# Dealing the seven VectorE steps of a float64 conversion differently over a unit, and testing the exponent with ScalarE's Square

## The chip, the cores and the metric

One core of one Trainium2 chip runs the program. The metric is the device time of one execution in microseconds (us); lower is better.

## What is computed

The reference is pooled attention, then a mixture of eight experts, then a layer with softplus. Cut to what matters:

```python
x = attention(q, mean_pool(k), mean_pool(v))          # x: 2304 x 512
P = sinkhorn(x @ moe_w_gate)                           # shares, 8 rounds
for e in range(8):
    out += P[:, e:e+1] * (np.maximum(x @ w1[e], 0) @ w2[e])
h = out @ moe2_w_in                                    # 512 x 2048
y = (np.maximum(h, 0) + np.log1p(np.exp(-np.abs(h)))) @ moe2_w_out
```

The two weights of the last layer arrive as float64. The kernel reads them as pairs of 32-bit words and turns them into float32 on the chip; that is the conversion which is changed here.

## The kernel before

**Precision and products.** Every float32 operand is split in a high and a low part, and each product is three matmuls (hi·hi, lo·hi, hi·lo; `three`, L797). The products of a unit are formed by a scheme with seven products in place of eight: A11, A22, S2, S1, A12, S3 and S4.

**Units and phases.** The 2304 tokens are worked on in three groups of 768. A unit is 256 columns of the hidden layer; an expert has four. There are six phases: the expert layer for the three groups (32 units each) and then the softplus layer for the three groups (8 units each). In the first phase and in the softplus phases each unit goes by itself (`first`, `second`). In the second and third phases (`TWICE`) units go in pairs, an even and an odd one: `first_twice` makes the hidden values of a unit, and the second product too is formed with seven products for the pair (`form_product`, from `second_twice`). The order in which the instructions are issued is written by hand, and each engine works its own list in that order: first(2d), second(2d−1), first(2d+1), second(2d), and so on.

**first_twice (L848).** It issues products A11, A22, S2, S1, A12 and S3, and later S4. After each of the first six it calls `between(k)`, k = 0 to 5. ScalarE copies A11's result to `za` between k = 0 and 1. VectorE forms `u1` (`u` in the trace) from S2's bank after S1 has been issued. S3 is accumulated onto that same bank, so S3 can't start before `u1` has been formed. After S3, VectorE makes three sums (`za` and two `p`), then comes `between(5)`. The posts of the unit follow in `second_twice`: `shared` (L889: relu times the shares), the high parts on ScalarE (L892) and the low parts on VectorE or GpSimd (L896), and sums (L845, L846).

**The conversion.** `from_float64` is a generator. One chunk is 128 x 512 values. `f` is the raw data: `up` the high words, `dn` the low words. Seven VectorE steps with a tile `a` (`da`), a tile `r` and a tile `t` (`dt`): shift and mask (L1258), put in sign and top exponent bit (L1260), shift the low word (L1264 or L1272), compare the magnitude and multiply (L1266), mask out the exponent (L1268), scale the low part (L1273), add (L1276). ScalarE's Abs (L1261) makes the magnitude in place in `f`, for the comparison of L1266. Each call of `convert()` runs the generator to its next `yield`, so a `yield` is where the next step waits for the next call. A `yield True` ends the chunk; then `done` stores `t`, and fetches the next raw data into `f`, at the next call of `settled()`.

In the pair phases `a` and `r` are the two halves of one double bank of PSUM on the side that the second products use (`not in_c`). `convert()` is called from `between(k)` of odd units, at k = 0 to 5, and only once a chunk is open after k = 0. So a chunk begins at k = 0 of an odd unit and its data is stored and the next fetched in the even unit that follows. In the other phases (`in_c`) the tiles are single banks, and `convert()` is called from `hook()`.

Tiles named "ex" (where `t` lives) have two buffers, which some remainders (`xl`) use as well.

Of the kernel before, what the change touches and what calls it, by code (L numbers as in the profile page):

```python
# [12 lines left out]
AF = mybir.ActivationFunctionType  # L13
ALU = mybir.AluOpType
# [5 lines left out]
def attention_moe_softplus_kernel(  # L20
# [12 lines left out]
    nc = tc.nc  # L33
# [46 lines left out]
    def bank(name, kind="y", dt=F32):  # L80
        if kind not in banks:
            kind = away[0] or ""
        if kind in halves:
            return banks[kind].tile([P, 2, 512], dt, tag=f"two{kind}", name=name)[:, 0, :]
        return banks[kind].tile([P, 512], dt, tag=f"bank{kind}", name=name)
# [1126 lines left out]
    def widths():  # L1212
        for u in range(NU2):
            o = u * US
            src = w_in[:, 2 * o:2 * (o + US)].rearrange("(c p) (f w) -> p c f w", p=P, w=2)
            for s in range(2):
                yield src[:, 2 * s:2 * s + 2], v1[u][:, 2 * s:2 * s + 2, :]
            src = w_out[o:o + US, :].rearrange("(c p) (d w) -> p c d w", p=P, w=2)
            for s in range(2):
                yield src[:, s:s + 1], v2[u][:, s:s + 1, :]  # L1220
# [6 lines left out]
    def from_float64():  # L1227

        ts, stt = nc.vector.tensor_scalar, nc.vector.scalar_tensor_tensor
        every = list(widths())  # L1230
        unread = list(enumerate(every))
        loaded = []

        def fetch(at):
            if unread and at < len(f64_t):
                i, (src, _) = unread.pop(0)
                _, c, f, w = src.shape
                raw = f64_t[at].rearrange("p (c f w) -> p c f w", c=c, w=w)
                nc.sync.dma_start(raw, src)
                loaded.append((i, at, raw))  # L1240

        for at in range(len(f64_t)):
            fetch(at)
        for _ in range(4):
            yield True
        while loaded:
            i, at, raw = loaded.pop(0)
            up = raw[:, :, :, 1].rearrange("p c f -> p (c f)")
            dn = raw[:, :, :, 0].rearrange("p c f -> p (c f)")
            size = lambda x: x.bitcast(F32)  # L1250
            in_c = "c" in banks
            if in_c:
                a = bank("da", "c", U32)
            else:
                both = banks[away[0]].tile([P, 2, 512], U32, tag=f"two{away[0]}", name="da")
                a, r = both[:, 0], both[:, 1]
            t = tpool.tile([P, up.shape[1]], F32, tag="ex", name="dt")
            ts(a, up, 3, 0x3FFFFFF8, op0=ALU.logical_shift_left, op1=ALU.bitwise_and)  # L1258
            yield False
            stt(a, up, 0xC0000000, a, op0=ALU.bitwise_and, op1=ALU.bitwise_or)  # L1260
            nc.scalar.activation(size(up), size(up), AF.Abs)  # L1261
            yield False
            if not in_c:
                ts(r, dn, 1, None, op0=ALU.logical_shift_right)  # L1264
            yield False
            stt(size(a), size(up), 1.125 * 2.0 ** -15, size(a), op0=ALU.is_ge, op1=ALU.mult)  # L1266
            yield False
            ts(t.bitcast(U32), a, 0xFF800000, None, op0=ALU.bitwise_and)  # L1268
            yield False
            if in_c:  # L1270
                r = bank("dr", "y", U32)
                ts(r, dn, 1, None, op0=ALU.logical_shift_right)  # L1272
            stt(t, r, 2.0 ** -51, t, op0=ALU.mult, op1=ALU.mult)  # L1273
            if in_c:
                yield False
            nc.vector.tensor_tensor(t, size(a), t, op=ALU.add)  # L1276

            def done(i=i, at=at, t=t):
                nc.sync.dma_start(every[i][1].rearrange("p c f -> p (c f)"), t)
                fetch(at)  # L1280
                converted[0] += 1

            settle.append(done)
            yield True


    conversion = from_float64()
    between_chunks = [True]

# [446 lines left out]
```

## Time and profile before

| | |
|---|---|
| median of 3 runs | 1968.52 us (1967.92 to 1969.78) |
| profiled execution | 1970.1 us, its span 1968.3 us |
| TensorE (PE) | busy 1936.8 us |
| VectorE (DVE) | busy 1465.7 us |
| GpSimd (POOL) | busy 1475.1 us |
| ScalarE (ACT) | busy 977.0 us |
| granted TensorE clock | 0.998 of full speed |

The span runs from the first to the last instruction of the profiled execution. Busy time says how much of it an engine had an instruction in work; a matmul's end is modelled, so a start that comes late against the pace of its neighbours says more than the busy time. In the rows below, what stands in square brackets is the time that the engine sat idle ahead of the instruction and the instruction that ended it.

### The profile page before, as it was taken

To read this page: it belongs to the slowest core of one execution; us is meant where nothing else is said; L and a number is where in the kernel's file an instruction comes from. 1 tells how busy PE (TensorE), PEld (TensorE's weight loads), DVE (VectorE), ACT (ScalarE), POOL (GpSimd) and SP (SyncE) were. 2 spreads that over 40 slices of the span, in tenths; PEclk is the share of its full clock that TensorE was granted. 3 is DMA by queue.
4 is the path that set the end of the run, shared out by engine and by line. 5 is a ranking of instruction groups with operands and counts; after the bars stand their busy time and mean duration, and the time that the engine had idled before them with its cause. 6 is when DMAs were issued, how large, how long until landed. Compare 5 with 4: busy or idle time off the path is not lost.

```text
span 1968.3 us, 30479 instructions
## 1 busy us (share of the span) xinstructions
PE 1936.8 (98%) x10954; PEld 1794.6 (91%) x10954; DVE 1465.7 (74%) x2339; ACT 977.0 (50%) x1777; POOL 1475.1 (75%) x1142
## 2 busy tenths in 40 slices
PE   9899999999999999999999999999999999999999
PEld 7677888888989999999999999999999988999998
DVE  6776576787667888878888879888789766556455
ACT  6545435343334545545445554454554565565542
POOL 5776667778877789778777798887787879666563
PEclk9999999999999999999999999999999999999999
DMA  7443433555547655554555655555545523523411
GB/s 198 120 147 125 144 124 135 177 166 182 179 153 262 200 164 166 166 181 152 160 172 159 214 169 163 160 170 162 186 150 158 190 85 115 202 91 115 139 65 64
DMA packets 213347, 306.56 MB, mean 156 GB/s; under 512 B 33308, under 2 KB 147532, under 8 KB 212940
## 3 DMA queue, kind: packets, MB, share of 16 engines
q1 hardware_dynamic: 203116, 290.85, 45.7%
q10 hardware_dynamic: 10080, 13.77, 1.9%
q8 instruction: 86, 1.41, 0.3%
q14 instruction: 65, 0.53, 0.1%
HBM read 239.30 MB, written 65.27 MB: 155 GB/s over the span
## 4 chain that ended last, share of the span: by engine, by line
PE 79%; DVE 14%; POOL 3%; ACT 3%; DMA 1%; issue 1%; SPq 0%; ACTq 0%; POOLq 0%; DVEq 0%
PE py L797 39%; PE p L797 36%; DVE p L889 2%; DVE g L845 2%; DVE hlo L896 2%; DVE p L845 2%; POOL w1lo L289 1%; ACT hhi L892 1%; DVE s L846 1%; DVE dt L1276 1%; PE px L522 1%; DVE dt L1273 1%; PE s L477 1%; DVE za L845 1%; DVE u L845 1%
## 5 line engine op out<-in xcount | busy, mean ns | idle before, releaser
L797 PE MATMUL p<-xhi,w1hi 128*128 128x384 f32 x1680 | 573.2, 341 | 10.0 <-DVE u L845 5.0
L797 PE MATMUL p<-xhi,w1lo 128*128 128x384 f32 x1680 | 563.7, 336 | 0.0
L797 PE MATMUL p<-xlo,w1hi 128*128 128x384 f32 x1680 | 563.5, 335 | 0.2 <-DVE xlo L1397 0.2
L289 POOL TENSOR_TENSOR w2lo<-w2raw,w2hi 128x512 fp32r<-128x512 f32 (+1 forms) x235 | 363.8, 1565 | 118.7 <-ACT w2hi L243 103.8
L289 POOL TENSOR_TENSOR w1lo<-w1raw,w1hi 128x512 fp32r<-128x512 f32 x240 | 239.3, 1019 | 232.9 <-ACT w1hi L320 232.1
L797 PEld LDWEIGHTS p<-xhi,w1hi 128*128 128x128 f32 x1680 | 315.9, 188 | 35.3 <-DVE u L845 14.3
L797 PEld LDWEIGHTS p<-xlo,w1hi 128*128 128x128 f32 x1680 | 316.0, 188 | 4.7 <-DVE xlo L1397 0.4
L797 PEld LDWEIGHTS p<-xhi,w1lo 128*128 128x128 f32 x1680 | 315.8, 188 | 0.0
L289 POOL TENSOR_TENSOR w1lo<-sums,w1hi 128x1024 fp32r<-128x1024 f32 x120 | 288.6, 2405 | 2.1 <-ACT w1hi L320 2.1
L797 PE MATMUL py<-w2hi,hhi 128*128 128x512 f32 x672 | 266.6, 397 | 5.4 <-DVE g L1117 1.6
L797 PE MATMUL py<-w2hi,hlo 128*128 128x512 f32 x672 | 263.8, 393 | 0.0
L797 PE MATMUL py<-w2lo,hhi 128*128 128x512 f32 x672 | 263.3, 392 | 0.0
L797 PE MATMUL py<-hhi,w2hi 128*128 128x384 f32 x716 | 241.4, 337 | 1.0 <-ACT whi L243 1.0
L797 PE MATMUL py<-hhi,w2lo 128*128 128x384 f32 x716 | 239.6, 335 | 0.0
L797 PE MATMUL py<-hlo,w2hi 128*128 128x384 f32 x716 | 239.5, 335 | 0.0
L845 DVE TENSOR_TENSOR g<-py,g 128x768 f32<-128x768 f32 x210 | 199.6, 950 | 50.1 <-PE py L797 50.1
L892 ACT CAST hhi<-p 128x768 fp32r<-128x768 f32 x128 | 102.6, 802 | 209.2 <-DVE p L889 174.6
L797 PEld LDWEIGHTS py<-w2hi,hhi 128*128 128x128 f32 x672 | 126.3, 188 | 36.9 <-DVE g L1132 4.5
L797 PEld LDWEIGHTS py<-w2hi,hlo 128*128 128x128 f32 x672 | 126.1, 188 | 26.9
L797 PEld LDWEIGHTS py<-w2lo,hhi 128*128 128x128 f32 x672 | 126.2, 188 | 22.2
L797 PEld LDWEIGHTS py<-hhi,w2hi 128*128 128x128 f32 x716 | 134.4, 188 | 5.1 <-DVE dt L1276 3.8
L797 PEld LDWEIGHTS py<-hhi,w2lo 128*128 128x128 f32 x716 | 134.5, 188 | 0.0
(164 smaller groups left out, 3548.1 us busy)
## 6 DMA issues: line engine op xcount, KB each, us to landing
w1raw<-in_moe_w_dram SPq DMA_DIRECT2D x96, 512.0 KB
w2raw<-td SPq DMA_DIRECT2D x128, 256.0 KB
sums<-sd SPq DMA_DIRECT2D x62, 512.0 KB
w2raw<-in_moe_w_dram SPq DMA_DIRECT2D x96, 256.0 KB
w2raw<-in_moe_w_dram SPq DMA_DIRECT2D x32, 512.0 KB
sd<-sums SPq DMA_DIRECT2D x32, 512.0 KB
td<-w2raw SPq DMA_DIRECT2D x64, 256.0 KB
xlo<-xlod SPq DMA_DIRECT2D x35, 384.0 KB
```

The costliest lines, as they stand in the source:

```text
L289: nc.gpsimd.tensor_tensor(o, a, b, op=ALU.subtract)
L477: nc.tensor.matmul(ps[:QP, j * 2 * SP:(j + 1) * 2 * SP], qT[:, j * QP:(j + 1) * QP], kb)
L522: nc.tensor.matmul(px[h * D:(h + 1) * D, :W], vp[:, h, :], aT[:, h, :])
L797: nc.tensor.matmul(ps, lhs[a], rhs[b], start=first and i == 0, stop=last and i == 2, skip_group_check=goes_on,)
L845: vadd = lambda o, x, y: nc.vector.tensor_tensor(o, x, y, op=ALU.add)
L846: vsub = lambda o, x, y: nc.vector.tensor_tensor(o, x, y, op=ALU.subtract)
L889: nc.vector.scalar_tensor_tensor(o, src, 0.0, share, op0=ALU.max, op1=ALU.mult)
L892: nc.scalar.copy(h_slot(q)[0], src)
L896: eng.tensor_tensor(lo, src, hi.bitcast(F32), op=ALU.subtract)
L1273: stt(t, r, 2.0 ** -51, t, op0=ALU.mult, op1=ALU.mult)
L1276: nc.vector.tensor_tensor(t, size(a), t, op=ALU.add)
```

## The change

In the pair phases, where a chunk had its VectorE steps dealt over six calls as 1, 1, 1, 1, 1, 2, it now has them dealt over five, as 2, 1, 2, 1, 1. In the other phases the seven steps stay dealt as they were (1, 1, 0, 1, 1, 2, 1). ScalarE's Abs, which stood behind the second step and wrote over the raw words, is replaced by a Square that is issued ahead of the first step and writes to `t`; the comparison reads `t` and compares with a squared bound. `t` is later overwritten by the masking step, as before.

```diff
+        least = (1.125 * 2.0 ** -15) ** 2 * (1 - 2.0 ** -23)
...
             t = tpool.tile([P, up.shape[1]], F32, tag="ex", name="dt")
+            nc.scalar.activation(t, size(up), AF.Square)
             ts(a, up, 3, 0x3FFFFFF8, op0=ALU.logical_shift_left, op1=ALU.bitwise_and)
-            yield False
+            if in_c:
+                yield False
             stt(a, up, 0xC0000000, a, op0=ALU.bitwise_and, op1=ALU.bitwise_or)
-            nc.scalar.activation(size(up), size(up), AF.Abs)
             yield False
             if not in_c:
                 ts(r, dn, 1, None, op0=ALU.logical_shift_right)
             yield False
-            stt(size(a), size(up), 1.125 * 2.0 ** -15, size(a), op0=ALU.is_ge, op1=ALU.mult)
-            yield False
+            stt(size(a), t, least, size(a), op0=ALU.is_ge, op1=ALU.mult)
+            if in_c:
+                yield False
             ts(t.bitcast(U32), a, 0xFF800000, None, op0=ALU.bitwise_and)
             yield False
             if in_c:
                 r = bank("dr", "y", U32)
                 ts(r, dn, 1, None, op0=ALU.logical_shift_right)
             stt(t, r, 2.0 ** -51, t, op0=ALU.mult, op1=ALU.mult)
-            if in_c:
-                yield False
+            yield False
             nc.vector.tensor_tensor(t, size(a), t, op=ALU.add)
```

## Rows read from the trace of the kernel before

**Rows 1.** The page's first part: busy time, share, instructions.

```profile
PE 1936.8 (98%) x10954; PEld 1794.6 (91%) x10954; DVE 1465.7 (74%) x2339; ACT 977.0 (50%) x1777; POOL 1475.1 (75%) x1142
```

**Rows 2.** Stretches: length, busy PE, PEld, DVE, ACT, POOL (instructions), clock, DMA share, GB/s.

```profile
1039.60:1069.60 30.00, 29.75 (x168) 29.01 (x169) 26.37 (x37) 14.40 (x24) 23.01 (x17) 1.00 0.55 171
...
1399.78:1429.19 29.41, 29.40 (x169) 29.08 (x169) 24.16 (x34) 15.73 (x27) 23.05 (x17) 1.00 0.53 174
```

**Rows 3.** Waits, whole span: us in total, times, longest us.

```profile
PEld p L797 <- DVE u L845: 14.3, 29, 0.6
...
PEld py L797 <- DVE dt L1276: 5.1, 23, 0.2
...
PE p L797 <- DVE u L845: 5.0, 21, 0.2
```

**Rows 4.** Timeline, VectorE, an odd unit with a chunk: start, us, instruction.

```profile
1052.39 0.96 DVE L845 TENSOR_TENSOR g<-py,g 128x768 f32<-128x768 f32 x1 [1.15 <-PE py L797]
1053.26 0.68 DVE L1258 TENSOR_SCALAR da<-f 128x512 uint32<-128x512 uint32 x1
1053.98 0.70 DVE L1260 SCALAR_TENSOR_TENSOR da<-f,da 128x512 uint32<-128x512 uint32 x1
1054.71 0.70 DVE L1264 TENSOR_SCALAR da<-f 128x512 uint32<-128x512 uint32 x1
1056.62 0.56 DVE L845 TENSOR_TENSOR u<-p,za 128x384 f32<-128x384 f32 x1 [1.21 <-PE p L797]
...
1059.22 1.03 DVE L845 TENSOR_TENSOR p<-p,za 128x384 f32<-128x384 f32 x2
1060.16 0.68 DVE L1273 SCALAR_TENSOR_TENSOR dt<-da,dt 128x512 f32<-128x512 uint32 x1
...
1061.49 0.96 DVE L889 SCALAR_TENSOR_TENSOR p<-p,pb 128x768 f32<-128x768 f32 x1
...
1069.00 0.55 DVE L845 TENSOR_TENSOR u<-p,za 128x384 f32<-128x384 f32 x1
```

**Rows 5.** Timeline, TensorE: start of S3, odd unit; around S3, next even unit.

```profile
1057.39 0.34 PE L797 MATMUL p<-xhi,w1hi 128*128 128x384 f32 x1
...
1069.02 0.34 PE L797 MATMUL p<-xhi,w1lo 128*128 128x384 f32 x1
1069.60 0.44 PE L797 MATMUL p<-xhi,w1hi 128*128 128x384 f32 x1 [0.25 <-DVE u L845]
1069.88 0.34 PE L797 MATMUL p<-xlo,w1hi 128*128 128x384 f32 x1
```

**Rows 6.** Timeline, VectorE, a stretch without a chunk: first post, next `u`.

```profile
1391.06 0.97 DVE L889 SCALAR_TENSOR_TENSOR p<-p,pb 128x768 f32<-128x768 f32 x1
...
1399.17 0.55 DVE L845 TENSOR_TENSOR u<-p,za 128x384 f32<-128x384 f32 x1
```

**Rows 7.** Timeline, ScalarE and VectorE: start of two odd units with a chunk.

```profile
1052.02 0.62 ACT L243 CAST whi<-w2raw 128x512 fp32r<-128x512 f32 x1 [1.45 <-DMA w2raw<-td]
1054.47 0.48 ACT L858 COPY za<-p 128x384 f32<-128x384 f32 x1 [1.83 <-PE p L797]
...
1204.43 0.68 DVE L1258 TENSOR_SCALAR da<-f 128x512 uint32<-128x512 uint32 x1
...
1205.88 0.62 ACT L243 CAST whi<-w2raw 128x512 fp32r<-128x512 f32 x1 [4.13 <-DMA w2raw<-td]
```

**Rows 8.** Groups of L1261, whole span: busy us, mean ns, idle before.

```profile
L1261 ACT ACTIVATE f<-f 128x512 f32<-128x512 f32 x32 | 21.8, 682 | 36.0 <-DVE da L1260 36.0
...
L1261 ACT ACT_TABLE_LOAD x2 | 2.6, 1283 | 0.0
```

**Rows 9.** Timeline, start of the softplus phases: VectorE, ScalarE, TensorE.

```profile
1612.39 0.70 DVE L1266 SCALAR_TENSOR_TENSOR da<-f,da 128x512 f32<-128x512 f32 x1 [0.75 <-ACT f L1261]
...
1618.81 1.28 ACT L817 ACT_TABLE_LOAD   x1 [0.98 <-DVE xl L741]
...
1624.99 0.50 PE L797 MATMUL py<-w2hi,hhi 128*128 128x512 f32 x1 [1.01 <-DVE g L1117]
```

## The prediction

> **What bounds the kernel now.** I read the engine totals first: TensorE is busy for 1936.8 us of a span of 1968.3 us [rows 1]. So only two things can change the time: the 31.5 us in which TensorE does nothing, and the places where its matmuls start later than their steady pace. Next I asked where conversion stands. The table of waits shows that in the two phases of pairs (units two by two) TensorE's weight loads wait 23 times for `dt`, the last result of a conversion chunk, 5.1 us in all, and 29 times for `u` (`u1` of `first_twice`), 14.3 us in all; its matmuls wait 21 times for `u`, 5.0 us [rows 3]. The reader is to see the counts: 23 is the number of chunks done in odd units.
>
> Then I compared stretches. A stretch from one S3 product of an even unit to the next holds 168 or 169 matmul records. With a chunk in it, it lasts 30.00 us; without, 29.41 us [rows 2]. TensorE has the same work in both, so a chunk costs TensorE 0.59 us. VectorE is busy for 26.37 us of the one and 24.16 us of the other, so it is not full in either: the chunk costs time because of where its steps stand in VectorE's queue.
>
> The timeline says where [rows 4]. Before `u` of the odd unit VectorE runs three steps (1053.26, 1053.98, 1054.71) and then idles 1.21 us until TensorE has the product. Two steps follow `u`, and two (1060.16 and the one behind it) stand after the odd unit's last sums `p`, ahead of `shared` (the first post, 1061.49), exactly where VectorE has no slack: from there to `u` of the next even unit (1069.00) it runs almost without a pause. TensorE's S3 product waits for that `u`: it starts 0.58 us after the matmul before it (1069.02, 1069.60) where 29.41 us over 169 matmuls [rows 2] make 0.17 the pace; 0.25 of it is idle, and the next start takes 0.28 [rows 5]. That is about 0.5 us lost at one place. The rest is the bank that the chunk holds until `dt` is added, and a first post 1.33 us late.
>
> **The change part by part.**
>
> *Steps dealt 2, 1, 2, 1, 1.* All seven VectorE steps remain, with their tiles. In an odd unit five stand ahead of `u` instead of three, two behind it, none after the last sums.
>
> Behind the sums [rows 4]: `shared` starts at 1060.16 instead of 1061.49, 1.33 us earlier. What that is worth at the next `u` I read from a stretch without a chunk, which has the same chain: `shared` at 1391.06, `u` at 1399.17, so 8.11 us [rows 6]. 1060.16 + 8.11 = 1068.27 against 1069.00: 0.73 us earlier. S3 started 0.60 us after `u` (1069.60 against 1069.00), so it could start at 1068.87. TensorE can't use more than it lost; the bound from both sides is nothing (another engine then holds S3) and 0.73. I take 0.59, the measured difference of the stretches, as TensorE then meets the same order as in a stretch without a chunk. The wait for `dt` (5.1 us over 23) is part of that difference and isn't added again.
>
> Ahead of `u`: two more steps must fit. A step that reads the result before it starts 0.04 us after that one ends (1053.26 + 0.68, then 1053.98); an independent one starts 0.09 before the end of its predecessor (1052.39 + 0.96, then 1053.26) [rows 4]. The comparison doesn't read the step ahead of it: 1054.71 + 0.70 − 0.09 = 1055.32. The mask does read it: 1055.32 + 0.69 + 0.04 = 1056.05. `u` is independent: 1056.05 + 0.69 − 0.09 = 1056.65 against 1056.62 now. So the idle 1.21 us is filled and `u` is 0.03 late. S3 of the odd unit starts at 1057.39 [rows 5]; with the 0.60 from above it needs `u` by 1056.79, so 0.14 us are left. I take no loss. If every added step took a dependent step's time, `u` would be another 0.26 late and S3 0.15.
>
> The two steps between `u` and the last sums replace two of the same length, so the last sums stay where they are.
>
> *Square for Abs.* One ScalarE instruction replaces another on 128x512 elements; the trace shows no Square, so its cost lies between the 0.48 us of the copy with 384 columns [rows 7] and the Abs's 0.68 with a table load of 1.28 on top [rows 8]; I take the Abs's own 0.68, the row with its shape. It no longer waits for VectorE: it reads the raw words, which were fetched in the even unit before, and writes a buffer of `t` whose last store belongs to an earlier stretch. But it now stands ahead of ScalarE's copy `za`, which would wait with it, and the comparison that reads it stands ahead of `u`. It must be ready by 1055.32, that is 2.06 us after the chunk's first step. In the stretch shown ScalarE is free after the `whi` cast at 1052.02 + 0.62 and idle until 1054.47, so Square ends near 1053.3: nothing lost. In one stretch of 21 the `whi` cast waited 4.13 us for its DMA and ended at 1206.50 [rows 7]; there Square would end near 1207.2, 2.8 after the first step (1204.43), and `u` would be 0.7 late. I charge 0.7 once.
>
> *The phases that step one by one* (bank "c") keep their dealing; only Square changes. Seven early chunks: ScalarE waited for VectorE there, but TensorE lost little. I take 0.3 us in all, with nothing and 1 us as ends. Two chunks fall at the start of the softplus phase. There Abs twice needs a table load [rows 8] and Softplus loads its table back (1618.81), 1.28 us each. TensorE then stands still for 1.01 us at 1624.99, waiting for `g` behind the late softplus [rows 9]. Without the loads: the first comparison no longer waits for Abs, which brings 0.4, an estimate from the second's 0.75; the second waited 0.75 us for it (1612.39 [rows 9]), so the chunk ends about 0.5 earlier, and with the 1.28 of the reload Softplus is 1.8 earlier. Sum 2.2 us; the ends are 0.9 (loads stay, only the wait goes) and 3.
>
> Does Square need those loads? No row shows it. The Trainium skill ("ScalarE: Activation LUTs", section "Table sets: the hidden batching unit") says that cheap functions, abs among them, are in every set. The trace disagrees: Abs behind Softplus loaded a table, 1283 ns, twice. By the page there would be nothing to save; by the row there is, if Square is served by Softplus's table.
>
> **The sum.** 21 stretches have the full pattern. 20 × 0.59 = 11.8; the one with the late cast 0.59 − 0.7 = −0.1. The two chunks at the phases' edges (23 − 21) have smaller waits: 0.7 together, an estimate from the `dt` wait (0.22) and the bank behind it. Softplus phase 2.2, early chunks 0.3. 11.8 − 0.1 + 0.7 + 2.2 + 0.3 = 14.9 us. The profiled execution took 1970.1 us with a span of 1968.3; its span would become 1953.4. The runs' median of 1968.52 lies 0.2 above that span, so 1968.5 − 15 = 1953.5 us.
>
> **The rivals.**
>
> *A. The odd unit's S3 becomes the stall.* The fit ahead of `u` has 0.14 us to spare. If steps run 0.1 slower, or Square is late in more stretches as TensorE gets faster and the w2 loads don't, S3 is 0.2 to 0.5 late in each of 21: 4 to 10 us go back, 1957.5 to 1963.5. For it: the slack is a computed one, and one cast is that late already [rows 7]. Against: the steps' rows differ by 0.02 [rows 4], and the stretches without a chunk get their `w2` loads in time at 29.41.
>
> *B. S3 of the even unit stays late.* If the posts on ScalarE or GpSimd hold it, only the `dt` waits (5.1) and the softplus phase (2.2) come off: 1961. Against: the stretches without a chunk run at 29.41 with the same posts.
>
> *C. Square loads tables as Abs did.* The 2.2 falls to 0.9: about 1955, inside the forecast's own range.
>
> *D. Slower: ScalarE holds up the comparison.* Place: the comparison, which now stands ahead of `u` and waits for Square, which waits behind ScalarE's `w2` casts and their DMAs. It decides from the point where Square ends 2.06 us after the chunk's first step; from there, less 0.14, each us late costs TensorE a us per stretch. To end slower by 4 us the 14.9 must be lost and 4 more, 0.9 us in each of 21 stretches, so Square ending 3.1 and the cast 2.4 us after the first step in all of them. The late one of the 21 ends 2.07 after it (1206.50, 1204.43) [rows 7].
>
> **Chances.** Forecast, with C in it: 0.72; A 0.12; B 0.09; D 0.03; something within 0.2% of no change beyond these, 0.04. Measurement can tell about 0.2%, 3.9 us, from no change. A and B are faster by more than that in nearly all of their span. Faster 0.90, same 0.06, slower 0.04. The likeliest case's own range is 1950.5 to 1957; for 8 in 10 I go up through A to B's 1961: 1950 to 1961. Below: the stretches can't become shorter than those without a chunk by what is shown, 21 × 0.14 more by the 0.73 bound is 3 us.
>
> **What would show it.** In the profile after: stretches between even S3 products of 29.4 to 29.5 us; five VectorE steps ahead of the odd `u` with almost no idle; `shared` straight behind the last sums; no wait of weight loads for `dt`; waits of matmuls for `u` nearly gone; one Softplus table load and none at Square. Wrong it is if the odd S3 shows a wait for `u`, or if the comparison waits for ScalarE in more than a few stretches.

## The result, and the profile after

The changed kernel takes 1954.07 us (median of 4 runs, 1953.51 to 1955.01); the kernel before, with them, 1968.36 (1967.92 to 1969.78). The ratio is 0.9919, with a 95% interval of 0.9906 to 0.9932: faster by 14.3 us, against a forecast of 15. The profiled execution took 1954.04 us with a span of 1952.3, at a granted clock of 0.999.

The first part of the page after, as [rows 1]:

```profile
PE 1928.6 (99%) x10954; PEld 1794.4 (92%) x10954; DVE 1471.4 (75%) x2339; ACT 973.6 (50%) x1773; POOL 1475.1 (76%) x1142
```

TensorE has the same 10954 matmuls; its idle time fell from 31.5 to 1952.3 − 1928.6 = 23.7 us, and the other 8 us are starts that come closer together. ScalarE has four instructions fewer, which are table loads.

Two stretches between even units' S3 products in the profile after, one with a chunk and one without, columns as in [rows 2]:

```profile
942.25:971.85 29.60, 29.59 (x168) 29.06 (x168) 26.70 (x37) 14.54 (x24) 22.98 (x17) 1.00 0.50 161
...
1387.30:1416.73 29.43, 29.42 (x168) 29.10 (x169) 24.16 (x34) 15.73 (x27) 23.05 (x17) 1.00 0.54 173
```

The stretch without a chunk is as it was; the one with a chunk fell from 30.03, which most of them last before (the 30.00 of [rows 2] is at the low end), to 29.60 and didn't reach it.

The waits after, as [rows 3]:

```profile
PEld p L797 <- DVE u L845: 14.0, 48, 0.6
...
DVE da L1268 <- ACT dt L1259: 3.2, 4, 1.0
...
PE p L797 <- DVE u L845: 0.2, 1, 0.2
```

TensorE's waits for `dt` are gone, and the matmuls' waits for `u` fell from 21 to 1. The weight loads wait for `u` 48 times instead of 29: the odd unit's `u` is now waited for too. New in the pair phases is the second row, the comparison waiting for ScalarE's Square, 4 times.

VectorE in an odd unit with a chunk and up to the next even unit's `u`, as [rows 4]:

```profile
1015.13 0.68 DVE L1260 TENSOR_SCALAR da<-f 128x512 uint32<-128x512 uint32 x1
1015.85 0.69 DVE L1263 SCALAR_TENSOR_TENSOR da<-f,da 128x512 uint32<-128x512 uint32 x1
1016.58 0.69 DVE L1266 TENSOR_SCALAR da<-f 128x512 uint32<-128x512 uint32 x1
1017.37 0.70 DVE L1268 SCALAR_TENSOR_TENSOR da<-dt,da 128x512 f32<-128x512 f32 x1
1018.10 0.69 DVE L1271 TENSOR_SCALAR dt<-da 128x512 uint32<-128x512 uint32 x1
1018.71 0.55 DVE L845 TENSOR_TENSOR u<-p,za 128x384 f32<-128x384 f32 x1
...
1021.27 1.03 DVE L845 TENSOR_TENSOR p<-p,za 128x384 f32<-128x384 f32 x2
1022.33 0.97 DVE L889 SCALAR_TENSOR_TENSOR p<-p,pb 128x768 f32<-128x768 f32 x1
1023.81 0.57 DVE L845 TENSOR_TENSOR p<-p,u 128x384 f32<-128x384 f32 x1 [0.51 <-PE p L797]
...
1030.46 0.55 DVE L845 TENSOR_TENSOR u<-p,za 128x384 f32<-128x384 f32 x1
```

Five steps stand ahead of the odd `u`, as forecast, and the first post (1022.33) stands straight behind the last sums. But `u` starts 1018.71 − 1015.13 = 3.58 us after the first step, where 3.36 was measured before and 3.39 forecast; and the step to look at is the fourth: the comparison starts 0.79 behind the shift step (1016.58, 1017.37) where 0.61 was forecast.

TensorE around the odd unit's S3 in the same stretch, as the first of [rows 5]:

```profile
1019.08 0.34 PE L797 MATMUL p<-xhi,w1lo 128*128 128x384 f32 x1
1019.31 0.44 PE L797 MATMUL p<-xhi,w1hi 128*128 128x384 f32 x1
1019.59 0.34 PE L797 MATMUL p<-xlo,w1hi 128*128 128x384 f32 x1
```

S3 starts 0.23 after its predecessor and the next matmul 0.28 after S3, where the pace is 0.17: 0.06 + 0.11 = 0.17 us lost, at a place where nothing was lost before.

### The profile page after: what moved, and what is told of

The parts are those of the page before. It is cut to its first block, busy times and chain, and to the rows that moved or that the text cites. A ratio compares the mean times of both kernels' runs of the same rounds, so it can differ in the third digit from the quotient of the medians.

```text
span 1952.3 us, 30469 instructions
## 1 busy us (share of the span) xinstructions
PE 1928.6 (99%) x10954; PEld 1794.4 (92%) x10954; DVE 1471.4 (75%) x2339; ACT 973.6 (50%) x1773; POOL 1475.1 (76%) x1142
## 4 chain that ended last, share of the span: by engine, by line
PE 90%; DVE 3%; POOL 2%; ACT 2%; DMA 1%; issue 1%; SPq 0%; ACTq 0%; DVEq 0%; POOLq 0%
PE py L797 45%; PE p L797 42%; POOL w1lo L289 1%; PE px L522 1%; PE s L477 1%; DMA vt<-in_v_dram 1%; PE pa L512 1%; DMA pb<-pd 0%; DVE p L1045 0%; POOL w2lo L289 0%; ACT w1hi L320 0%; DMA w2raw<-td 0%; PE pq L464 0%; ACT xhi L693 0%; DVE za L1045 0%
```

## The experiments

All are compared with the kernel before, timed beside them on the same chip (medians 1968.75 to 1970.1 us there). The changed kernel, run again so:

> The changed kernel once more, beside the next three on one chip: 14 to 16 us under the kernel before.

Measured 1955.46 us, 0.9926 [0.9909, 0.9943].

**Each half alone.** The dealing of before with the Square:

```diff
+            nc.scalar.activation(t, size(up), AF.Square)
             ts(a, up, 3, 0x3FFFFFF8, ...)
...
-            nc.scalar.activation(size(up), size(up), AF.Abs)
...
-            stt(size(a), size(up), 1.125 * 2.0 ** -15, ...)
+            stt(size(a), t, least, ...)
```

> The Square alone, with the steps dealt as before. If the two edits work apart, as I now read the two traces: the early chunks (about 2 us) and the softplus phase (2.3 us) come off, the stretches with a chunk stay at 30.0 us: about 1964. If freeing ScalarE from its wait for VectorE is the whole cause, 1954. If the dealing is the whole cause, 1968.

Measured 1964.74 us, 0.9969 [0.9956, 0.9981]. A stretch of it with a chunk:

```profile
1009.84:1039.88 30.04, 29.79 (x168) 29.05 (x168) 26.49 (x37) 14.44 (x24) 22.98 (x17) 1.00 0.53 160
```

The Square does nothing for the pair phases; its gain lies elsewhere. The new dealing with the Abs (after, with this edit):

```diff
-            nc.scalar.activation(t, size(up), AF.Square)
...
             stt(a, up, 0xC0000000, a, ...)
+            nc.scalar.activation(size(up), size(up), AF.Abs)
...
-            stt(size(a), t, least, ...)
+            stt(size(a), size(up), 1.125 * 2.0 ** -15, ...)
```

> The dealing alone; Abs stays, behind the second step. If the two edits work apart: stretches with a chunk of 29.6 us in place of 30.0, 21 x 0.43 = 9 us off and a little at the edges, two table loads at Abs stay: 1958 to 1960. If the Square is the whole cause, 1968; if the dealing is, 1954. Abs ends some 2.1 us after the chunk's first step and stands ahead of the copy za, so a wait of the comparison for it would show here too: then above 1960.

Measured 1961.22 us, 0.9952 [0.9939, 0.9965]. A stretch of it, and one of its waits:

```profile
1004.87:1034.47 29.60, 29.59 (x169) 29.06 (x169) 26.70 (x37) 14.54 (x24) 23.04 (x17) 1.00 0.53 161
```

```profile
ACT f L1263 <- DVE da L1262: 68.6, 26, 6.7
```

The stretch is that of the full change, though ScalarE waits longer for VectorE than before (68.6 us in 26 waits against 36.0, [rows 8]); those waits hurt mostly outside the pairs. In four of the 21 stretches in the pairs the comparison does wait for the Abs, 0.5 to 2.5 us, and they last 29.76 to 30.27. The product of the ratios is 0.9969 × 0.9952 = 0.9921, the ratio of both together 0.9919: within the intervals, the halves add.

**Abs back in the unit-by-unit phases alone.**

```diff
-            nc.scalar.activation(t, size(up), AF.Square)
+            if not in_c:
+                nc.scalar.activation(t, size(up), AF.Square)
...
+            if in_c:
+                nc.scalar.activation(size(up), size(up), AF.Abs)
```

The comparison reads `size(up)` against the old bound in these phases again.

> As after, but Abs comes back in the phases that step unit by unit (7 early chunks, 2 in the softplus phase). If Abs cost 1.8 us in the early chunks and 2.3 us at the softplus phase: 4 us more, 1958; two table loads at Abs come back. If the early difference of the two traces is scatter of the first 100 us: 2.3 us more, 1956.4. If it is hidden everywhere: 1954.

Measured 1960.71 us, 0.9948 [0.9934, 0.9961]; its span is 1958.0, 5.7 more than that of after. By the starts of the same matmuls 2.3 of it come between 331 and 500 us, in the early chunks, and 2.3 in the softplus phase; 1.0 lies at the start, ahead of any chunk. What the early chunks lose stands in the trace of before, ScalarE and TensorE:

```profile
390.49 0.66 ACT L1261 ACTIVATE f<-f 128x512 f32<-128x512 f32 x1 [6.71 <-DVE da L1260]
...
392.83 0.50 PE L797 MATMUL py<-w2hi,hhi 128*128 128x512 f32 x1 [0.54 <-DVE g L1132]
...
394.98 0.50 PE L797 MATMUL py<-w2hi,hhi 128*128 128x512 f32 x1 [0.49 <-DVE g L1132]
```

The Abs sat 6.71 us in ScalarE's queue waiting for VectorE's second step; the relu casts `hhi` stood behind it, and TensorE waited twice, about half a us each, for the `g` that follows them. In after the Square waits for no VectorE step and these two waits are gone.

**Why the odd `u` is late.** Theory: `a` and `r` are halves of one tile, so the comparison, which reads and writes `a`, waits until the shift step has written `r`. Rival: the five steps are slow for another reason. A tile of its own for `r`:

```diff
-                a, r = both[:, 0], both[:, 1]
+                a = both[:, 0]
+                r = tpool.tile([P, up.shape[1]], U32, tag="ex", name="dr")
```

> As after, but the shifted low word r goes to an SBUF tile of its own, not to the other half of the double bank that holds a. If the comparison starts 0.79 us after the r step because both are halves of one tile: it starts 0.1 to 0.18 earlier, u at 3.41 to 3.5 us after the first step in place of 3.59, the odd unit's S3 loses some 0.05 us in place of 0.19: 21 x 0.13 = 2.7 us less, about 1951.5. If the gap only comes from the comparison's second wait (for ScalarE), nothing changes: 1954.

Measured 1999.5 us, 1.0151 [1.0133, 1.0169]. This was a miss on both sides: 45 us slower than after. The shift step now reads and writes SBUF alone. Its group, then VectorE, GpSimd and TensorE around the first long one:

```profile
L1267 DVE TENSOR_SCALAR dr<-f x23: 418/421/9780, 633.3 to 1563.6; 128x512 uint32<-128x512 uint32 x23
```

```profile
721.41 8.09 DVE L1267 TENSOR_SCALAR dr<-f 128x512 uint32<-128x512 uint32 x1
...
729.42 0.68 DVE L1269 SCALAR_TENSOR_TENSOR da<-dt,da 128x512 f32<-128x512 f32 x1
```

```profile
719.44 3.80 POOL L289 TENSOR_TENSOR w2lo<-w2raw,w2hi 128x512 fp32r<-128x512 f32 x3
...
726.88 2.34 POOL L289 TENSOR_TENSOR w1lo<-sums,w1hi 128x1024 fp32r<-128x1024 f32 x1
```

```profile
731.35 0.69 PE L797 MATMUL p<-xhi,w1hi 128*128 128x384 f32 x1 [6.96 <-DVE u L845]
```

The median shift takes 0.42 us, less than in PSUM (0.69), but five of the 23 take 8.1 to 9.8. The first long one starts while GpSimd works through seven instructions back to back (719.44 to 729.22) and ends at 729.50, 0.28 after the last of them. TensorE stands still for 6.96 us, and from 731.35 to 735.35 its granted clock is 0.50, the lower of its two levels (1.2 GHz):

```profile
731.35:735.35 4.00, 4.00 (x13) 4.00 (x14) 2.84 (x6) 0.00 (x0) 0.00 (x0) 0.50 0.19 74
```

The five stalls sum to 34.4 us, and at a mean clock of 0.54 in the 4 us behind each, 5 × 4 × 0.46 = 9.2 more are lost: 43.6 of the 45. The Trainium skill ("SBUF — State Buffer", section "Who interferes with whom") says that a VectorE instruction with at most one SBUF input and outside its two-port modes does not contend with GpSimd, and that one in such a mode, as `tensor_scalar` may be, shuts GpSimd out or is shut out. The trace agrees that the two exclude each other; the page says that the loser waits for one whole instruction, and in these five cases it waited for a row of them.

Back-to-back work of GpSimd is not enough for that. Of the 18 short shifts 17 also start while GpSimd works, nearly all in a run of its instructions; 13 of them take 0.42 to 0.44 us and 4 take 0.80 to 0.88. One of the 13, with GpSimd around it:

```profile
691.98 0.42 DVE L1267 TENSOR_SCALAR dr<-f 128x512 uint32<-128x512 uint32 x1
...
690.82 1.29 POOL L289 TENSOR_TENSOR wlo<-w2raw,whi 128x512 fp32r<-128x512 f32 x1
692.07 1.48 POOL L289 TENSOR_TENSOR w2lo<-w2raw,w2hi 128x512 fp32r<-128x512 f32 x1
```

It ends 0.30 after the GpSimd instruction that was in work, and the next one takes 1.48 instead of 1.29. All 22 shifts that meet GpSimd end 0.28 to 0.30 after the end of one of its instructions: the 17 after the one in work, the five after a row. What decides between the two isn't shown.

To have the separate tile without that form of step, the shift step was given a PSUM operand. It ors `a` into `r`, so in the pair phases the converted weights are not the reference's:

```diff
-                ts(r, dn, 1, None, op0=ALU.logical_shift_right)
+                stt(r, dn, 1, a, op0=ALU.logical_shift_right, op1=ALU.bitwise_or)
```

> As the kernel with r in an SBUF tile of its own, but the shift step also reads the PSUM tile a (its result is the shifted word or-ed with a, so the converted weights are not the reference's in the chunks of the pair phases). If the five waits of 8 us come from a step with its one source and its destination in SBUF, which can't run while GpSimd works: none is left, the step takes 0.69 and not 0.42 us, about 1952 to 1956. If they come from r taking one of the two buffers of its tag, the waits stay: 1995 to 2000.

Measured 1974.13 us, 1.0019 [1.0008, 1.0031]. VectorE in the same unit, and the group of its shift step:

```profile
720.44 0.69 DVE L1267 SCALAR_TENSOR_TENSOR dr<-f,da 128x512 uint32<-128x512 uint32 x1
721.05 0.69 DVE L1269 SCALAR_TENSOR_TENSOR da<-dt,da 128x512 f32<-128x512 f32 x1
...
722.38 0.55 DVE L845 TENSOR_TENSOR u<-p,za 128x384 f32<-128x384 f32 x1
722.84 5.91 DVE L1277 SCALAR_TENSOR_TENSOR dt<-dr,dt 128x512 f32<-128x512 uint32 x1
```

```profile
L1267 DVE SCALAR_TENSOR_TENSOR dr<-f,da x23: 686/686/690, 632.3 to 1536.5; 128x512 uint32<-128x512 uint32 x23
```

The time lies between the two forecasts, but the rows settle two things. With `r` in another tile the comparison starts 0.61 behind the shift step, and `u` 3.38 after the first step (which starts at 719.00), as the prediction had worked it out (3.39). The odd unit's S3 then loses nothing: it and the next matmul start 0.17 after the ones before them. A stretch with a chunk, in which GpSimd delays no step:

```profile
1006.04:1035.49 29.45, 29.44 (x168) 29.11 (x169) 26.60 (x37) 14.55 (x24) 23.50 (x17) 1.00 0.57 164
```

That is the length without a chunk, so the shared tile is what delays `u` in after and costs the 0.17. And no shift step is long any more, though `r` still takes a buffer of the same tag, so the long ones came with the step that touches SBUF alone. The total is no gain, because now the scale step, whose inputs both lie in SBUF, takes 5.5 to 5.9 us in three stretches (here it ends at 728.75, 0.55 after GpSimd's run), and TensorE waits for the sums behind it, 12.1 us in three waits; these stretches last 35.8 to 36.3, together 19.6 us more. Of the places tried, the PSUM halves cost least, 0.2 us.

**Where the steps stand.** One step moved from ahead of the odd `u` to behind it, 2, 1, 1, 2, 1:

```diff
             stt(size(a), t, least, ...)
-            if in_c:
-                yield False
+            yield False
             ts(t.bitcast(U32), a, 0xFF800000, ...)
-            yield False
+            if in_c:
+                yield False
```

> As after, with the steps dealt 2, 1, 1, 2, 1: four ahead of the odd u, three between it and the last sums. If the fifth step ahead of u is what holds the odd unit's S3 (it now starts some 0.06 late and restarts 0.11 slow): u back at 3.36 us after the first step and that loss gone, about 0.17 us in each of 21 stretches; but the third step behind u makes the last sums some 0.35 late, and the even S3 has no slack: 0.28 becomes 0.6. Net 2 to 4 us slower than after. If the even side has slack, 3.5 us faster than after.

Measured 1951.22 us, 0.9900 [0.9885, 0.9916]. Once more:

> The dealing 2, 1, 1, 2, 1 once more, beside the next two: 4 to 5 us under the changed kernel, so 18 to 20 us under the kernel before.

Measured 1951.28 us, 0.9907 [0.9889, 0.9924]. It is the fastest version, 2.8 to 4.2 us below the two medians of after; the intervals of the ratios overlap, and it is the stretches that carry the difference. One of them, and its VectorE:

```profile
1029.31:1058.77 29.46, 29.45 (x168) 29.13 (x168) 26.62 (x37) 14.54 (x24) 22.99 (x17) 1.00 0.56 174
```

```profile
1016.88 0.56 DVE L845 TENSOR_TENSOR u<-p,za 128x384 f32<-128x384 f32 x1 [0.41 <-PE p L797]
...
1021.06 0.97 DVE L889 SCALAR_TENSOR_TENSOR p<-p,pb 128x768 f32<-128x768 f32 x1
1022.05 0.57 DVE L845 TENSOR_TENSOR p<-p,u 128x384 f32<-128x384 f32 x1
```

`u` is back at 3.35 after the first step (1013.53) and waits for TensorE again; three steps now stand between `u` and the last sums. The instruction behind the first post, which in after idled 0.51 us for TensorE, follows here without a wait: the later sums have used up nearly all of that. In the profile of the first run the 21 stretches are 12.1 us shorter than before, 0.58 each, against 8.2 us in after. How far that goes was tried with four steps behind the odd `u`, 2, 1, 0, 3, 1:

```diff
+            if not in_c:
+                yield False
             stt(size(a), t, least, ...)
             if in_c:
                 yield False
             ts(t.bitcast(U32), a, 0xFF800000, ...)
-            yield False
+            if in_c:
+                yield False
```

> Dealt 2, 1, 0, 3, 1: three steps ahead of the odd u as before the change, four between it and the last sums, none behind them. In the 2, 1, 1, 2, 1 dealing the sum p<-p,u follows the first post without idle, so the 0.51 us that VectorE spent waiting for S4 there is used up. If so, the fourth step behind u (0.72 us) reaches the even u in full: 0.6 to 0.7 us in each of 21 stretches, 12 to 15 us slower than 2, 1, 1, 2, 1, about 1963. If there is more slack behind the sums, 1950.

Measured 1965.86 us, 0.9983 [0.9972, 0.9994]. A stretch of it, and the even unit's first product:

```profile
1027.77:1057.88 30.11, 29.71 (x169) 29.07 (x169) 26.64 (x37) 14.55 (x23) 22.99 (x16) 1.00 0.58 171
```

```profile
1057.88 0.45 PE L797 MATMUL p<-xhi,w1hi 128*128 128x384 f32 x1 [0.39 <-DVE p L845]
```

One step more behind `u` costs 0.65 us per stretch, not at the even `u`, as expected, but at the sums that the even unit's first product waits for. The slack behind the sums is that of one step, not of two.

**The even unit's S3.** In after it still starts 0.36 after its predecessor and the next 0.28 after it, 0.3 us lost in each stretch, with a chunk or without. One of the even unit's posts was moved behind its `u`:

```diff
-        for _ in range(2):
+        for _ in range(1):
```

> As after, with one of the two posts that stand ahead of the even unit's u (the subtraction p<-p,s of 0.97 us) issued behind it. If the even S3 waits for u only because of VectorE's queue, u comes 0.87 earlier, and the 0.28 us that each even S3 still loses go, with a chunk or without: some 30 x 0.28 = 8 us faster than after, stretches of 29.3 with a chunk. If the bank that the post frees is what comes next, the first second product of the odd unit waits instead, and nothing is gained.

Measured 1968.23 us, 0.9989 [0.9977, 1.0]. A stretch of it, and the second product behind:

```profile
1037.63:1067.62 29.99, 29.65 (x168) 29.11 (x168) 26.81 (x37) 14.54 (x24) 23.01 (x16) 1.00 0.56 174
```

```profile
1037.63 0.44 PE L797 MATMUL py<-hhi,w2hi 128*128 128x384 f32 x1 [0.34 <-DVE a L845]
```

`u` comes in time, but the next second product waits for the sum `a`, which now stands behind the late post: a new wait, dearer than the one removed.

**The shift step first** (the place in the chain changed, not the dealing):

```diff
             nc.scalar.activation(t, size(up), AF.Square)
+            if not in_c:
+                ts(r, dn, 1, None, op0=ALU.logical_shift_right)
             ts(a, up, 3, 0x3FFFFFF8, ...)
```

> As after, with the shift of the low word as the first of the seven steps, so that the comparison does not follow it. If the comparison waits for whatever wrote the double bank last, the five steps ahead of u take the same or up to 0.15 us less (one dependence fewer in the chain), u at 3.4 to 3.6 us: 0 to 3 us faster than after. If the two halves were tracked apart, u would be at 3.4 and S3 lose nothing: 3 us faster.

Measured 1956.62 us, 0.9929 [0.9914, 0.9945], with a stretch of 29.63 us: no difference from after. The step behind it starts 0.73 later, so the wait on the shared tile only moved. The comparison now stands behind a step whose result it does read:

```profile
1022.59 0.69 DVE L1264 SCALAR_TENSOR_TENSOR da<-f,da 128x512 uint32<-128x512 uint32 x1
1023.38 0.70 DVE L1268 SCALAR_TENSOR_TENSOR da<-dt,da 128x512 f32<-128x512 f32 x1
```

It starts 0.79 behind it, the same as in after behind a step whose result it doesn't read.

## Why the prediction was right, and where its terms were not

The terms can be read as the shift of the same matmul's start from before to after.

| matmul before → after | shift, us | what lies since the row above | forecast |
|---|---|---|---|
| 99.67 → 97.35 | 2.3 | the start | none |
| 620.00 → 615.26 | 4.7 | early chunks: 2.4 | 0.3 (0 to 1) |
| 651.72 → 646.50 | 5.2 | the first edge chunk: 0.5 | 0.7 for two |
| 1548.69 → 1534.93 | 13.8 | 21 stretches: 8.2; the second edge chunk: 0.4 | 11.7 |
| the spans' ends | 16.0 | softplus: 2.3 | 2.2 |

Outside the start this is 13.7 us against 14.9. The 2.3 at the start isn't a gain of the change: two profiles of the version 2, 1, 1, 2, 1, whose medians agree to 0.1, have spans of 1948.2 and 1955.4, and differ there (this matmul starts at 97.30 and 104.49). The medians, 14.3 apart, are the better measure of the whole. That the total came so close is luck: two errors of size, −3.5 and +2.1, have opposite signs.

*The stretch (the mechanism right, the term too large).* Forecast 0.59 us for each, measured 0.43 (30.03 to 29.60). All 21 give 8.2: the one with the late cast became 0.3 longer, where 0.1 was forecast, and the other 20 are 8.5 shorter. The step that failed is "the comparison doesn't read the step ahead of it: 1054.71 + 0.70 − 0.09". It doesn't read it, but `r` is written into the other half of the same tile, and it was made to wait: 0.79 instead of 0.61. [rows 4] had shown it: the shift step, which reads only `f`, starts 0.73 behind the step ahead of it (1053.98, 1054.71), as a dependent step does, and not 0.61. The text had priced that (`u` "another 0.26 late and S3 0.15") and took no loss; `u` is 0.23 late and TensorE loses 0.17. The remainder: 29.41 + 0.17 = 29.58 of the 29.60. This is rival A, a little below its smallest size: 0.17 × 20 = 3.4 us. By the prediction's own sign ("Wrong it is if the odd S3 shows a wait for `u`") this step was wrong, though the total lay in its range. With `u` early again, in 2, 1, 1, 2, 1, the 21 stretches do give 12.1 us, 0.4 more than the 11.7 forecast.

*No slack behind the sums (true before, not after).* The prediction read VectorE as running "almost without a pause" from the sums to the next `u`. In the trace before it does. With the posts 1.33 us earlier, VectorE idles 0.51 us for TensorE behind the first post, and the stretch without a chunk from which the prediction took its 8.11 us has the same pause:

```profile
1392.52 0.57 DVE L845 TENSOR_TENSOR p<-p,u 128x384 f32<-128x384 f32 x1 [0.50 <-PE p L797]
```

So the sum held it already. What the text didn't ask is whether a step could stand there at no cost: one can, as the version with three steps behind `u` shows, and a second can't (0.65 us per stretch).

*The even unit's S3.* That it falls back to the stretch without a chunk held: its matmul no longer idles for `u`. Rival B had no part in it. The 0.3 us that the stretch without a chunk loses there too weren't to be had by a later post.

*The late cast (charged once, right in this profile).* It happened in one stretch, and in another to a smaller degree (29.80 us). The other two of the four waits for Square, 1.01 us each, stand ahead of a `u` that waits for TensorE anyway. In the profile of the repeat no stretch with a full pattern lasts over 29.81, so that just one came here is chance. ScalarE, then VectorE of the first:

```profile
750.46 0.62 ACT L243 CAST whi<-w2raw 128x512 fp32r<-128x512 f32 x1 [4.46 <-DMA w2raw<-td]
750.99 0.66 ACT L1259 ACTIVATE dt<-f 128x512 f32<-128x512 f32 x1
...
751.68 0.70 DVE L1268 SCALAR_TENSOR_TENSOR da<-dt,da 128x512 f32<-128x512 f32 x1 [0.85 <-ACT dt L1259]
```

The chain of rival D is seen whole here, cast, Square, comparison, and at its price: TensorE's starts at 752.07 and 753.62 come 0.29 and 0.40 late, with 0.1 more at each restart 0.9 in all, where the other odd units lose 0.17; 0.7 more, as charged.

*Square's price and its table.* The groups of Square and of the table loads at Softplus in after:

```profile
L1259 ACT ACTIVATE dt<-f 128x512 f32<-128x512 f32 x32 | 21.5, 672 | 0.0
...
L817 ACT ACT_TABLE_LOAD x1 | 1.3, 1283 | 0.0
```

Square takes 672 ns against the 682 of [rows 8], the value taken, and loads no table; Softplus loads its own once. So rival C fell. The softplus term, 2.2, came from three rows and measured 2.3.

*The early chunks (too small by eight times).* "ScalarE waited for VectorE there, but TensorE lost little" was said without following what is queued behind the Abs. The row at 390.49, its 6.71 us and the two waits of TensorE behind it were in the trace.

## What to carry to other kernels

A step dealt into an engine's pause must be priced with every dependency that the tile, not the data, gives it: two halves of one tile made two independent steps wait for each other. Moving such a step out of the tile is not free either; a VectorE step that touches SBUF alone waited in 5 of 23 cases behind a whole run of GpSimd's, so look at what GpSimd does at that moment. And of a wait on an in-order queue, price what stands behind it: the Abs cost nothing itself in the early chunks, the casts behind it did.

## What the runs showed of the hardware that was not expected

- A VectorE shift from SBUF to SBUF, 128x512, took 0.42 us, but 8.08 to 9.78 in 5 of 23 cases. These five began while GpSimd ran instructions back to back; 17 of the others also began while it worked, nearly all in such a run, and took 0.88 at most; why the five waited longer is open. With one input in PSUM it was 0.69 in all 23. That GpSimd is what holds it is read from the ends that agree; no run removed GpSimd's work.
- After a matmul of 384 columns that comes 0.06 to 0.4 us late, the next start takes 0.28 instead of 0.17: each short stall costs 0.11 more than it shows.
